# Two transpositions by DMA earlier on their queue, and one step's PSUM transposes later and copied by another engine

## The chip, the cores and the metric

The kernel runs on one core of one Trainium2 chip. The metric is the device time of one execution in microseconds (us). Before the change three executions took 198.18, 198.23 and 198.60 us, median 198.23.

## What is computed

A lightning attention block with decay, followed by a dense layer with a tanh GELU:

```python
# q, k, v: (4, 8, 768, 64); lam: (8,); blocks of 64 rows, kv_state starts at zero
intra = einsum('bhic,bhjc->bhij', qb, kb) * Dmask      # Dmask[i,j] = lam**(i-j), i >= j
intra = einsum('bhij,bhjd->bhid', intra, vb)
inter = einsum('bhid,bhde->bhie', qb * lam_pow, kv_state)
out[:, :, block] = intra + inter
kv_state = lam_block * kv_state + einsum('bhsd,bhse->bhde', kb * rev_pow, vb)
...
x = out.transpose(0, 2, 1, 3).reshape(3072, 512)
h = x @ w_in                                           # w_in: (512, 2048)
g = 0.5 * h * (1 + tanh(sqrt(2/pi) * (h + 0.044715 * h**3)))
result = g @ w_out                                     # w_out: (2048, 512)
```

Inputs and output are float32; the kernel computes in float16 with float32 accumulation.

## The kernel before

The attention is cut into 24 steps. A step is one batch, 256 rows and four of the eight heads; its three loads (q, k, v, 256 KB each) go out in `load_step` (L60, DMA at L70). `cast_q` (L277) scales the queries to float16 on VectorE (L282), `cast_k` (L290) casts the keys on ScalarE (L295), `scale_v` (L264) scales the values on GpSimd (L266). Queries and keys must then be transposed so that the head dimension lies on the partitions. Up to step 7 TensorE does that into a PSUM tile `Tps` (`stage_t`, L309, matmuls at L321), and ScalarE or VectorE copies it to `qkT` (L325 to L330). From step 8 on (`FIRST_DMA_T`) it is a transposing DMA on SP's queue (`transpose_dma`, L299, L303), which here is called T8, T9 and so on by its step.

`scores` (L344) computes a step's scores S (L350), `causal` (L356) masks them on VectorE into PT (L360). `products` (L365) makes the K products for the state (L385), those of PT with v (L400) and those with the state (L413, L422). `burst` (L437) does the same for two steps at once: scores of both (four PSUM banks), O products (L460, two banks), K products (L475, two banks, `K0` and `K1`), then the products with the state (L488, L498). `update` (L535) carries the state: t on VectorE (L547, L550), u on GpSimd (L558, L565). `x_out` (L514) takes the attention's result to `xT` on ScalarE (L527, L529).

The dense layer is cut into seven groups of steps and each group into pieces in a list `filler`: `mm1` (L609) makes `Hps` in PSUM (L613) and has ScalarE apply the GELU to `gT` (L617); `mm2` (L622) makes `O2ps` (L628), copied out by ScalarE (L636); later groups use `product` (L668, matmuls at L692) and `seven` (L778, L791) with sums on VectorE (L662). `fill(n)` (L958) issues the next n pieces.

The order of the work is written out by hand from L988 to L1190: each engine, and SP's queue of DMAs, works through its own instructions in that order (`pin` keeps it). `R(n, s)` (L962) issues the scores of step n with the products of steps n and s; `U(n)` (L984) the second state update. `fill` calls put dense pieces between them. From step 8 to 12 a loop over `FILL` (L1083) does this; `prep_qk(n + 2)` (L269) in it casts and transposes two steps ahead, and loads run up to four steps ahead. Behind the loop stand `burst((13, 14), (12,))`, with six dense `Hps` pieces between step 16's casts and it, and `burst((15, 16), (13, 14))`.

All PSUM tiles come from one pool of eight banks (`ps_M`, L55); a bank is given out again when the last reader of its former tile is done. The buffers of the loads are four per name (`ld`, L45), those of `qkT` five (`qkp`, L47).

Of the kernel before, what the change touches and what calls it, by code (L numbers as in the profile page):

```python
# [15 lines left out]
def kernel(  # L16
# [43 lines left out]
    def load_step(s, names="qkv"):  # L60
        b, r = divmod(s, 2 * NSB)
        sb, half = divmod(r, 2)
        ts = ld32.setdefault(s, [])
        for nm, src in (("q", q), ("k", k), ("v", v)):
            if nm not in names:
                continue
            t = ld.tile([P, HH, 2, D], FP32, tag=nm + "32", name=f"{nm}32_{s}")
            rows = src[b, half * HH : (half + 1) * HH, sb * SB : (sb + 1) * SB, :]
            queue = nc.scalar if (nm, s) == ("v", 0) else nc.sync
            pin(queue.dma_start(out=t[:].rearrange("p h j d -> p h (j d)"),  # L70
                                in_=rows.rearrange("h (p j) d -> p h (j d)", j=2)))
            ts.append(t)
# [71 lines left out]
    def sum_win(m, j, eng):  # L144

        if not wi_sum:
            wi_sum.extend(wst.tile([P, 2, 2, DFF // 2], FP16, tag=f"w{2 + i}", name=f"ws{i}")
                          for i in range(2))
        a, op, b = I_SUMS[m]
        cs, fs = slice(0, 2), slice(512 * j, 512 * j + 512)  # L150
        pin(eng.tensor_tensor(w_in_block(m, cs, fs), w_in_block(a, cs, fs),
                              w_in_block(b, cs, fs), op))
# [92 lines left out]
    def prep(s):  # L245
        prep_qk(s)
        prep_v(s)
# [16 lines left out]
    def scale_v(s):  # L264
        tv = a16p.tile([P, 2, HH, D], FP16, tag="v16", name=f"v16_{s}")
        pin(nc.gpsimd.tensor_tensor(wide(tv[:]), ld32[s][2][:], decay(dv, s), ALU.mult))  # L266
        a16[s] = a16[s] + (tv,)

    def prep_qk(s):  # L269
        cast_qk(s)  # L270
        transpose_dma(s)

    def cast_qk(s):
        cast_q(s)
        cast_k(s)

    def cast_q(s):  # L277
        q32 = ld32[s][0]
        tqk = a16p.tile([P, 2, 2, HH, D], FP16, tag="qk16", name=f"qk16_{s}")
        tq, tk = tqk[:, 0], tqk[:, 1]  # L280
        q_eng = nc.gpsimd if s == 3 else nc.vector
        pin(q_eng.tensor_tensor(wide(tq), q32[:], decay(dq, s), ALU.mult))  # L282
        if s == 0:
            inverse(halves[0])
            odd(halves[1])
            inverse(halves[1])
        a16[s] = (tq, tk)
        whole_qk[s] = tqk

    def cast_k(s):  # L290
        tk, k32 = a16[s][1], ld32[s][1]
        if s == 4:
            pin(nc.vector.tensor_copy(out=wide(tk), in_=k32[:]))
        else:
            pin(nc.scalar.activation(out=wide(tk), in_=k32[:], func=AF.Copy))  # L295
# [3 lines left out]
    def transpose_dma(s):  # L299
        tqk = whole_qk.pop(s)  # L300
        if s >= FIRST_DMA_T:
            o = qkp.tile([P, 2, 2, 2, P], FP16, tag="qkT", name=f"qkT_{s}")
            pin(nc.sync.dma_start_transpose(out=o[:].rearrange("p a j h t -> p (a j h) t"),  # L303
                                            in_=tqk[:].rearrange("p a j h d -> p (a j h d)")))
            qkT[s] = o
            if s == FIRST_DMA_T + 1:
                load_step(s + 1, "v")

    def stage_t(s):  # L309
        if s >= FIRST_DMA_T:  # L310
            return
        tq, tk = a16[s][:2]
        if s < 4:
            Tps = [ps_M.tile([P, 2, 2, P], FP16, tag="M", name=f"Tps{i}") for i in range(2)]
        else:
            Tps = ps_M.tile([P, 2, 2, 2, P], FP16, tag="M", name="Tps")
        for i, t in enumerate((tq, tk)):
            to = Tps[i] if s < 4 else Tps[:, i]
            for hp in range(2):
                for j in range(2):  # L320
                    pin(nc.tensor.transpose(to[:, j, hp, :], t[:, j, 2 * hp : 2 * hp + 2, :],  # L321
                                            ident[:]))
        o = qkp.tile([P, 2, 2, 2, P], FP16, tag="qkT", name=f"qkT_{s}")
        if s < 4:
            pin(nc.scalar.activation(out=o[:, 0], in_=Tps[0][:], func=AF.Copy))  # L325
            pin(nc.vector.tensor_copy(out=o[:, 1], in_=Tps[1][:]))
        elif s in (5, 6, 8):
            pin(nc.scalar.activation(out=o[:], in_=Tps[:], func=AF.Copy))
        else:
            pin(nc.vector.tensor_copy(out=o[:], in_=Tps[:]))  # L330
        qkT[s] = o
# [12 lines left out]
    def scores(n):  # L344
        o = qkT[n]
        Sps = [ps_M.tile([P, 2, 2, P], FP32, tag="M", name=f"S{hl}") for hl in range(2)]
        for hp in range(2):
            for jk in range(2):
                for hl, c in TILES:
                    pin(nc.tensor.matmul(  # L350
                        Sps[hl][half64(c), hp, jk, :], o[half64(hl), 1, jk, hp, half64(c)],
                        o[half64(hl), 0, :, hp, half64(c)], start=True, stop=True,
                        skip_group_check=True))
        Ss[n] = Sps

    def causal(n):  # L356

        t = ptp.tile([P, 2, 2, 2, P], FP16, tag="PT", name=f"PT_{n}")
        for hl, Sps in enumerate(Ss.pop(n)):
            pin(nc.vector.tensor_tensor(  # L360
                t[:, hl].rearrange("p b c d -> p b (c d)"), Sps[:].rearrange("p b c d -> p b (c d)"),
                mask[:].unsqueeze(1).to_broadcast([P, 2, 2 * P]), ALU.mult))
        PTs[n] = t
# [227 lines left out]
    def store_pair(pair):  # L591
        rows = out[2 * pair * P : 2 * pair * P + 2 * P, :].rearrange("(i p) d -> p i d", p=P)
        for i in range(2):
            pin(nc.sync.dma_start(out=rows[:, i], in_=o_pairs[pair][:, i]))
# [363 lines left out]
    def fill(n):  # L958
        for _ in range(min(n, len(filler))):
            filler.pop(0)()  # L960

    def R(n, s, ahead=None, keep=False):  # L962

        def first():
            if n is not None:
                scores(n)
            if ahead:
                ahead()

        if s in NARROW:  # L970
            products(n, s, between=first)
        else:
            first()
            products(n, s)
        if n is not None:
            causal(n)
        if s is not None and s % 2 == 1:
            g, i = group_of[s // 2]
            if i == len(groups[g]) - 1 and g > 0:
                queue_group(g)  # L980
        if n is not None and not keep:
            update(n, 0)

    def U(n):  # L984
        update(n, 1)


    idle(2, 512)  # L988
    prep(0)
    stage_t(0)  # L990
    chunk_decay()
    idle(1)
    prep(1)
    R(0, None)
    idle(0, 384)
    stage_t(1)
    idle(3)
    U(0)
# [3 lines left out]
    causal(1)  # L1002
    idle(2)
    stage_t(2)
    prep_qk(3)
    update(1, 0)
# [49 lines left out]
    sum_wout(1, 2, DVE)  # L1056
    fill(2)
    R(4, None)
    stage_t(5)
    U(4)  # L1060
    prep(6)
    fill(2)
    R(5, 4)
    stage_t(6)
    U(5)
# [18 lines left out]
    for n, (a, b, c, d) in FILL.items():  # L1084
        stage_t(n)
        fill(a + (n == 10))
        if n == 8:
            cast_q(n + 2)
            fill(1)
            cast_k(n + 2)  # L1090
            transpose_dma(n + 2)
        else:
            prep_qk(n + 2)
        if n < 11:
            load_step(n + 4, "qkv" if n < 10 else "qk")
        if n == 9:
            store_pair(1)
        if n == 11:
            scale_v(13)
            load_step(14, "v")  # L1100
            load_step(16, "qk")
        elif n == 9:
            scale_v(11)
        elif n == 10:
            scale_v(12)
            load_step(15, "qk")
        elif n == 12:
            scale_v(14)
        fill(b + (n == 8) - (n == 10))
        R(n, n - 1, keep=n == 8)  # L1110
        fill(c)
        if n == 8:
            update(n, 0)
            scale_v(n + 2)
            fill(2)
        U(n)
        if n == 12:
            prep_qk(15)
            load_step(15, "v")
            load_step(16, "v")  # L1120
            scale_v(15)
        fill(d)
        if n > 8:
            sum_win((n - 7) // 2, (n - 1) % 2, nc.vector)

    cast_qk(16)
    load_step(17, "qk")
    transpose_dma(16)
    load_step(17, "v")
    while kept_stores:  # L1130
        kept_stores.pop(0)()
    scale_v(16)
# [86 lines left out]
```

## Time and profile before

| What | Value |
|---|---|
| Time, median of three executions | 198.23 us (198.18 to 198.60) |
| Profiled execution | 198.31 us, its span 196.5 us |
| TensorE (PE) | 189.7 us busy, 97% of the span |
| VectorE (DVE) | 145.7 us, 74% |
| ScalarE (ACT) | 126.0 us, 64% |
| GpSimd (POOL) | 68.1 us, 35% |
| Mean granted TensorE clock | 0.997 of full speed |
| DMA | 38.13 MB, mean 194 GB/s |

The profile is of one execution on the chip; its times count from the start of the span. Lines as L613 are lines of the kernel. In a list by time each line has the start, the length, the engine, the operation with output and input, a count, and in brackets the engine's idle time before it with what ended that. SPq is the queue on which SP issues DMAs: its lengths are the time to issue, not to transfer; a transfer's end is its landing. The chain of waits is the work that ended last, followed back from the end; a list of waits gives, for an engine and line and what it waited for, the total in us, the number of times and the longest. Ends of matmuls are modelled, so that their starts say more than their busy share.

### The profile page before, as it was taken

What the parts mean: (1) busy time and instruction counts of PE and PEld (TensorE: products, weight loads), DVE (VectorE), ACT (ScalarE), POOL (GpSimd) and SP (SyncE); (2) the same over time, 40 slices, a digit from 0 to 9 for tenths busy, and PEclk for the clock granted to TensorE, in tenths of its full rate; (3) what the DMA queues carried; (4) which work ended last, traced back from release to release, by engine and by line L of the source; (5) the groups of instructions that cost most, each with busy time, mean ns of one, the idle gap of its engine ahead of it and who ended that gap; (6) DMA issues with size and microseconds to landing.
All of it is one profiled execution on the core that took longest, in us unless ns stands there. A gap on an engine that the chain in (4) does not pass through costs nothing.

```text
span 196.5 us, 5992 instructions
## 1 busy us (share of the span) xinstructions
PE 189.7 (97%) x2469; PEld 138.7 (71%) x2469; DVE 145.7 (74%) x291; ACT 126.0 (64%) x250; POOL 68.1 (35%) x85
## 2 busy tenths in 40 slices
PE   8878999999999999999999999999999999999992
PEld 2546544456888888654688754578888888888882
DVE  4987732889989879949889926999557996487520
ACT  3673778357774796686856379844877856678211
POOL 6594213557444732068524416064002030002000
PEclk9999999999999999999999999999999999999998
DMA  6999999999999999999997999600520300021105
GB/s 168 291 322 385 386 386 387 298 286 295 255 218 237 262 343 219 213 217 302 256 275 169 266 307 156 146 4 0 47 87 29 110 5 0 3 107 45 65 29 184
DMA packets 62810, 38.13 MB, mean 194 GB/s; under 512 B 18624, under 2 KB 55744, under 8 KB 62784
## 3 DMA queue, kind: packets, MB, share of 16 engines
q1 hardware_dynamic: 62240, 37.50, 76.8%
q8 instruction: 19, 0.31, 0.7%
q10 hardware_dynamic: 544, 0.26, 0.5%
q14 instruction: 7, 0.06, 0.1%
HBM read 27.26 MB, written 6.29 MB: 171 GB/s over the span
## 4 chain that ended last, share of the span: by engine, by line
PE 89%; SPq 4%; DMA 4%; ACT 0%; issue 0%
PE Hps L613 25%; PE MX L692 18%; PE MY L692 9%; PE HX L791 7%; PE O2ps L628 7%; PE MW L692 4%; DMA wi<-in_moe_w_in_dram 4%; SPq L70 4%; PE HY L791 4%; PE S L350 3%; PE Hps L890 3%; PE HW L791 2%; PE O L460 1%; PE OK L400 1%; PE Tps L321 1%; PE OK L422 1%
## 5 line engine op out<-in xcount | busy, mean ns | idle before, releaser
L613 PE MATMUL Hps<-xT,w_in 128*128 128x512 f16 (+1 forms) x288 | 50.5, 332 | 0.0
L613 PEld LDWEIGHTS <-w_in 128*128 128x128 f16 x288 | 27.8, 98 | 19.4
L617 ACT ACTIVATE gT<-Hps 128x512 f16<-128x512 f32 x56 | 32.6, 597 | 9.1 <-PE Hps L613 8.7
L360 DVE TENSOR_TENSOR PT<-S,mask 128x512 f16<-128x512 f32 x48 | 30.3, 680 | 8.6 <-PE S L350 8.6
L692 PEld LDWEIGHTS <-gs 128*128 128x128 f16 x320 | 31.1, 98 | 3.7
L266 POOL TENSOR_TENSOR v<-v,dv 128x512 f16<-128x512 f32 x24 | 27.5, 1150 | 17.3 <-DMA v<-in_v_dram 17.1
L692 PEld LDWEIGHTS <-gT 128*128 128x128 f16 x240 | 23.2, 98 | 3.5 <-ACT gT L617 0.2
L565 POOL TENSOR_TENSOR u<-t,lumask 128x256 f16<-128x256 f32 x21 | 15.2, 737 | 22.6 <-DVE t L550 13.6
L692 PE MATMUL MX<-w_sum,gs 128*128 128x256 f16 x160 | 21.4, 273 | 0.0
L662 DVE TENSOR_TENSOR gs<-gT 128x1024 f16<-128x1024 f16 (+1 forms) x24 | 17.2, 722 | 3.0 <-ACT gT L617 3.0
L282 DVE TENSOR_TENSOR qk<-q,dq 128x512 f16<-128x512 f32 x23 | 18.3, 798 | 1.2 <-DMA q<-in_q_dram 1.1
L295 ACT ACTIVATE qk<-k 128x512 f16<-128x512 f32 x23 | 14.4, 625 | 7.2 <-DMA k<-in_k_dram 7.1
L744 POOL TENSOR_TENSOR o<-u,q 128x512 f32<-128x512 f32 (+1 forms) x5 | 6.1, 1212 | 37.0 <-ACT u L709 37.0
L558 POOL TENSOR_TENSOR u<-t,lamu 128x128 f16<-128x128 f32 x19 | 10.7, 572 | 21.3 <-DVE t L550 15.7
L628 PE MATMUL O2ps<-w_out,gT 128*128 128x512 f16 x64 | 14.6, 379 | 0.0
L791 PEld LDWEIGHTS <-ws 128*128 128x128 f16 x128 | 12.4, 98 | 1.6 <-DVE xs L770 0.2
L529 ACT ACTIVATE xT<-OK 128x256 f16<-128x256 f32 x22 | 8.7, 453 | 6.7 <-PE OK L422 3.1
L709 ACT ACTIVATE u<-MX 128x256 f32<-128x256 f32 x18 | 6.9, 383 | 7.4 <-PE MX L692 7.4
L628 PEld LDWEIGHTS <-gT 128*128 128x128 f16 x64 | 6.1, 98 | 6.6
L692 PE MATMUL MY<-w_out,gs 128*128 128x256 f16 x80 | 10.7, 273 | 0.0
L805 DVE COPY u<-HX 128x512 f32<-128x512 f32 x8 | 5.5, 689 | 6.8 <-ACT gT L809 4.4
L692 PE MATMUL MX<-w_sum,gT 128*128 128x256 f16 x80 | 10.4, 273 | 0.0
(105 smaller groups left out, 322.0 us busy)
## 6 DMA issues: line engine op xcount, KB each, us to landing
q<-in_q_dram SPq DMA_DIRECT2D x24, 256.0 KB, 5.0
k<-in_k_dram SPq DMA_DIRECT2D x24, 256.0 KB, 5.1
v<-in_v_dram SPq DMA_DIRECT2D x23, 256.0 KB, 5.2
out_dram<-o SPq DMA_DIRECT2D x23, 256.0 KB, 4.1
wo<-in_moe_w_out_dram SPq DMA_DIRECT2D x4, 1024.0 KB, 9.5
wi<-in_moe_w_in_dram SPq DMA_DIRECT2D x4, 512.0 KB, 8.2
wi<-in_moe_w_in_dram SPq DMA_DIRECT2D x2, 1024.0 KB, 12.8
v<-in_v_dram ACTq DMA_DIRECT2D x1, 256.0 KB, 4.3
```

The lines of the kernel that those rows point to most:

```text
L266: pin(nc.gpsimd.tensor_tensor(wide(tv[:]), ld32[s][2][:], decay(dv, s), ALU.mult))
L282: pin(q_eng.tensor_tensor(wide(tq), q32[:], decay(dq, s), ALU.mult))
L295: pin(nc.scalar.activation(out=wide(tk), in_=k32[:], func=AF.Copy))
L360: pin(nc.vector.tensor_tensor(t[:, hl].rearrange("p b c d -> p b (c d)"), Sps[:].rearrange("p b c d -> p b (c d)"), mask[:].unsqueeze(1).t ...
L558: pin(nc.gpsimd.tensor_tensor(u, state[half][:], lamu[:, 2 * half : 2 * half + 2].unsqueeze(2).to_broadcast([P, 2, D]), ALU.mult))
L565: pin(nc.gpsimd.tensor_tensor(u[:], state[half][:].unsqueeze(2).to_broadcast([P, 2, 2, D]), lumask[:, 2 * half : 2 * half + 2, :].unsqueez ...
L613: pin(nc.tensor.matmul(by_block(Hps[:, i, :]), w_in16[:, c, f * P : (f + 1) * P], x(c), start=(c == 0), stop=(c == NC - 1)))
L617: pin(nc.scalar.activation(out=dst, in_=Hps[:], func=AF.Gelu_apprx_tanh))
L628: pin(nc.tensor.matmul(O2[tau][0][:], gT[:, f % HF, f // HF, tau * P : (tau + 1) * P], w_out16[:, f, :], start=(n == 0), stop=(n == NF - 1)))
L662: pin(nc.vector.tensor_tensor(g_rows(m, i), g_rows(a, i), g_rows(b, i), op))
L692: pin(nc.tensor.matmul(dst, lhsT, rhs, start=(opens and i == 0), stop=(closes and i == HF - 1), skip_group_check=True))
L791: pin(nc.tensor.matmul(dst[:, i, :], w_in_block(a, slice(c, c + 1), slice(f * P, f * P + P))[:, 0], x_block(b, slice(c, c + 1))[:, 0], sta ...
```

## The change

Two things are done.

First, step 5. Its transposes on TensorE (`stage_t(5)`) stood right behind `R(4, None)`, with two dense pieces between them and the scores of step 5 and none before. Now one of these two pieces stands ahead of the transposes and one behind. The copy of step 5's `Tps` to `qkT` goes from ScalarE (L328) to VectorE (L330). (Step 8, which the old condition named too, is transposed by DMA and does not come here.)

Second, SP's queue of DMAs. The load of q and k of step 16 was issued in the loop's round 11, behind the load of v of step 14; now it is issued in round 12, behind the transposition of step 14. And the transposition of step 16 stood behind the load of q and k of step 17; now it stands ahead of it, right behind the casts of step 16. On SP's queue:

```
before: T13, v14, q16, k16, T14, T15, v15, v16, q17, k17, T16, v17
after:  T13, v14, T14, q16, k16, T15, v15, v16, T16, q17, k17, v17
```

On ScalarE and VectorE the casts of steps 14 to 17 keep their places among the other instructions.

```diff
@@ stage_t
-        elif s in (5, 6, 8):
+        elif s == 6:
             pin(nc.scalar.activation(out=o[:], in_=Tps[:], func=AF.Copy))
         else:
             pin(nc.vector.tensor_copy(out=o[:], in_=Tps[:]))
@@ the order of the work
     R(4, None)
+    fill(1)
     stage_t(5)
     U(4)
     prep(6)
-    fill(2)
+    fill(1)
     R(5, 4)
@@ in the loop over FILL
         if n < 11:
             load_step(n + 4, "qkv" if n < 10 else "qk")
+        elif n == 12:
+            load_step(16, "qk")
...
         if n == 11:
             scale_v(13)
             load_step(14, "v")
-            load_step(16, "qk")
@@ behind the loop
-    cast_qk(16)
-    load_step(17, "qk")
-    transpose_dma(16)
-    load_step(17, "v")
+    prep_qk(16)
+    load_step(17)
```

## The prediction

> **What bounds the kernel now.** I read the page's chain first, then TensorE's waits, then the stretches that the change touches. A step is one q, k, v triple; T14 stands for step 14's transposition by DMA, S for scores.
>
> ```profile
> PE 89%; SPq 4%; DMA 4%; ACT 0%; issue 0%
> ```
>
> The chain is TensorE (PE) nearly throughout; the SP and DMA shares lie in the first 18 us. TensorE's waits:
>
> ```profile
> PE S L350 <- DVE qkT L326: 0.8, 2, 0.5
> ...
> PE OK L422 <- POOL u L565: 0.5, 1, 0.5
> ```
>
> These and the others listed lie before 20 us. From 20 to 193 us TensorE is busy without a break, so there is almost nothing for a reordering to gain, and any new stall is added to the end. The one trace of a wait is in the chain in order of time (start, length, what):
>
> ```profile
> 86.98 0.67 PE S L350 x32
> ...
> 87.88 0.28 PE K L475 x32
> ...
> 93.56 0.57 PE S L350 x32
> ```
>
> Both S lines are 32 equal matmuls, of steps 13/14 and 15/16. The first takes 0.10 more: between S13 and S14 the starts stand 120 ns apart where others stand 46. S14's weight loads begin at 87.24; T14's last semaphore increment is at 87.19. So T14 comes 0.07 us late. T16 landed at 92.59, 1.2 us before S16 needs it.
>
> ScalarE before that burst:
>
> ```profile
> 84.43 0.60 ACT L617 ACTIVATE gT<-Hps 128x512 f16<-128x512 f32 x1 [0.27 <-PE Hps L613]
> 85.03 0.63 ACT L295 ACTIVATE qk<-k 128x512 f16<-128x512 f32 x1
> 85.57 1.19 ACT L617 ACTIVATE gT<-Hps 128x512 f16<-128x512 f32 x2
> 87.02 0.60 ACT L617 ACTIVATE gT<-Hps 128x512 f16<-128x512 f32 x1 [0.27 <-PE Hps L613]
> ```
>
> The second line casts step 16's keys (k16). Three gelus are queued behind it. The last ends at 87.62, and the program's waits name it: K1, the second PSUM bank of the burst's K products (L475), is the bank that gelu empties. K starts at 87.71. That margin is 0.09 us, less the 0.05 that a release takes elsewhere (T14's increment to S14's load).
>
> SP's queue, and k16's landing counted from its issue:
>
> ```profile
> 76.00 3.43 SPq L303 DMA_TRANSPOSE qkT<-qk  x1
> 79.47 0.58 SPq L70 DMA_DIRECT2D v<-in_v_dram  x1
> 80.10 0.51 SPq L70 DMA_DIRECT2D q<-in_q_dram  x1
> 80.65 0.55 SPq L70 DMA_DIRECT2D k<-in_k_dram  x1
> 81.36 3.32 SPq L303 DMA_TRANSPOSE qkT<-qk  x2
> ```
>
> ```profile
> DMA to landing us min/median/max: 4.4/4.4/4.4
> ```
>
> The order is T13, v14, q16, k16, T14 and T15. k16 landed at 80.65 + 4.36 = 85.01 and its cast began at 85.03: ScalarE had no slack left for it. The DMA engines in these stretches (last two columns: DMA share, GB/s):
>
> ```profile
> 84.30:85.25 0.95, 0.95 (x6) 0.42 (x5) 0.74 (x1) 0.82 (x2) 0.95 (x2) 1.00 1.27 280
> ...
> 85.70:87.00 1.30, 1.30 (x12) 0.48 (x14) 0.00 (x0) 1.04 (x2) 0.86 (x2) 1.00 1.02 9
> 87.00:87.50 0.50, 0.50 (x36) 0.43 (x40) 0.12 (x1) 0.48 (x1) 0.00 (x0) 1.00 1.21 268
> ```
>
> T14's 256 KB move in the first stretch. T15 then moves half its packets and halts for 1.3 us, though it had been issued by 84.69. What precedes a halted transposition has its increments held too: T14, whose data had moved by 85.25, reports at 87.19; k15, just ahead of the halting T13, landed 6.2 us after its issue instead of 4.4. By their packets twelve of the sixteen transpositions halt so; T14, T16, T18 and T19 do not (first to last packet 1.0 to 1.9 us instead of 1.7 to 2.8).
>
> [...] landings follow SP's order, 0.85 to 0.95 us apart. [...] a cast that waits for its load holds the gelus behind it. The list above is consistent with that; no long such wait is in this stretch. [...]
>
> **Step 5's transposes later.** Eight transposes (L321) swap places with one piece of four O2ps matmuls (4 x 0.216 = 0.86 us): nothing is added on TensorE. The ScalarE copy (L328, 1.025 us) goes; VectorE gets a copy (L330) in its place:
>
> ```profile
> 41.92 1.27 DVE L360 TENSOR_TENSOR PT<-S,mask 128x512 f16<-128x512 f32 x2
> 43.12 0.46 DVE L550 SCALAR_TENSOR_TENSOR t<-t,lamu,OK 128x64 f32<-128x64 f32 x2
> 43.50 0.68 DVE L282 TENSOR_TENSOR qk<-q,dq 128x512 f16<-128x512 f32 x1
> ```
>
> ```profile
> L330 DVE COPY qkT<-Tps x2: 690/691/692, 39.8 to 50.7; 128x1024 f16<-128x1024 f16 x2
> ```
>
> The transposes now start near 42.75 and end near 43.36. VectorE, busy since 40.51, reaches the copy at 43.50, where step 6's query cast started. It ends at 44.19; a release takes 0.05 (the early copies of L326 show it), so S5 loads at 44.24 instead of 44.16: +0.08 us. Between 0 (were VectorE earlier) and 0.3. On VectorE step 6's cast and PT of step 5 follow some 0.2 to 0.7 late; 0.45 us of idle before PT takes up most. PT5's products are at 47.7, PT then ready at 46.1; step 6's transposes at 45.1, its queries then ready at 44.9. ScalarE's removed microsecond ends nobody's wait.
>
> **Transpositions sooner.** T14 is issued after v14, at 80.10 instead of 81.36, ahead of q16 and k16; its casts were done at 79.76. On the compute engines no instruction of these steps changes place, on GpSimd's queue nothing at all; v15, v16 and T15 keep theirs on SP. T14 lands before 86 or so: S14's 0.07 us go. T16 passes q17 and k17, and T16's input depends on k16. S16 had 1.2 us of slack; q17 and k17 slip by about 1 us, and their casts stood at 92.53 (landed 90.92) and 94.09 (landed 91.78): covered, still more so if TensorE is late.
>
> The cost: k16 is now behind T14 in the ring, so its data come at least one transposition (0.95 us) later. They then take the place directly ahead of T15, which T14 held. The DMA total up to there is unchanged. If T15 halts as before, k16 reports when T14 did, at 87.19. ScalarE then casts at 87.2; from cast start to the end of the third gelu are 0.54 + 3 x 0.60 = 2.34 us, so K1's bank is free at 89.54 and K1 starts at 89.59 instead of 87.71: +1.88 us. S5's 0.08 disappears in this wait, because the DMA sets its end. O1 and K0 wait for the first two of these gelus and come in under it. Nothing later gives it back, TensorE having no idle.
>
> The sum is made against the profiled execution: 198.31 us, of which 196.5 are its span and 1.8 lie around it. 198.31 + 1.9 = 200.2. The median shown is 0.08 lower: 200.1.
>
> **Rivals.** (a) Likeliest: exactly one of T14 and T15 halts ahead of k16's report; 200.1, bounds 199.6 to 200.6; 0.44. (b) Both halt: for it, twelve of sixteen halt and T14 now starts closer behind its issue; against it, T14 did not. k16 then reports 1.3 us later still: 201.4; 0.22. (c) Neither: k16 at 85.96, K1 at 85.98 + 2.34 + 0.05 = 88.37: +0.66, 198.9; 0.11. (d) T13 does not halt or the whole DMA stream runs about 1.3 us earlier: k16 reports by 85.3, and the third gelu is again held by its matmuls only: 198.1 to 198.5; 0.17. (e) The other side: T14's lateness is the point. In the trace it costs 0.07 us; were T14 commonly late by a further halt (1.3 us, TensorE waiting from 87.15 on), its removal would give 196.9 to 197.8. It decides from a T14 landing after 87.5. Against it, profiled and unprofiled times differ by only 0.08 us; 0.06.
>
> **How the numbers follow.** Some 0.2% (0.4 us) is about what can be told from no change. Slower: (a), (b), (c), 0.77. Same: (d), 0.17. Faster: (e), 0.06. The likeliest case is 200.1. The range goes from the middle of (d), 198.3, to that of (b), 201.4; it leaves out (e), half of (d) and the upper part of (b), together 0.2. The halt is the unknown cost, 0 or 1.3 us for each of two transpositions, and I take one.
>
> **What would show it.** Right: on ScalarE a wait of about 2 us for k at L295 near 85; K at L475 starting near 89.6; S of steps 13/14 down to 0.57 in the chain; S5 some 0.1 late. Wrong: the cast of k16 starting by 85.3, or TensorE passing K without a gap. The whole is wrong if the gelu that K1 waits for was issued ahead of the cast.

## The result, and the profile after

The changed kernel takes 200.59 us, the median of six executions (199.93 to 202.29), beside 198.34 for the kernel before (six, 198.17 to 198.60). The ratio is 1.013 (95% interval 1.0088 to 1.0173): slower, clear of the noise. A second set of six, e8_after below, gave 201.24 (200.02 to 202.39), ratio 1.014 (1.0101 to 1.0179). The ratios in this document leave out executions over 1.5% above the fastest of their kernel, one of e3_t16 and four of e5_v15_between. The profiled execution took 200.44 us, 2.13 more than that of before; its span is 198.7.

The page's chain, after:

```profile
PE 87%; DMA 5%; POOL 2%; SPq 2%; ACT 1%; issue 1%; ACTq 0%; POOLq 0%
```

TensorE lost two points of the chain. POOL's share lies in the first 14 us; where the kernel differs, the chain in order of time (start, length, what) is:

```profile
82.73 4.97 DMA k<-in_k_dram
...
87.72 0.63 ACT qk L295
88.35 1.47 ACT gT L617 x3
...
89.86 0.44 PE K L475 x31
...
95.70 0.57 PE S L350 x32
```

The chain no longer runs through TensorE here. It runs from the load of k16 to its cast, through the three gelus behind the cast, and to the K product that needs the bank of the third. K1 starts at 89.86, not 87.71: +2.15. The scores of steps 15/16 start at 95.70, not 93.56: +2.14. In this execution the distance stays from here to the end; nothing is given back. ScalarE's list says the same:

```profile
87.72 0.63 ACT L295 ACTIVATE qk<-k 128x512 f16<-128x512 f32 x1 [1.89 <-DMA k<-in_k_dram]
88.26 1.55 ACT L617 ACTIVATE gT<-Hps 128x512 f16<-128x512 f32 x3
```

The bracket is the idle time ahead of the cast, ended by the load. Before, this cast began at 85.03 with none. TensorE's list at the same place, before and then after:

```profile
86.91 0.74 PE L350 MATMUL S<-qkT 64*64 64x128 f16 x32
87.48 0.39 PE L460 MATMUL O<-PT,v 64*64 64x128 f16 x16
87.71 0.45 PE L475 MATMUL K<-v,qk 64*64 64x64 f16 x32
```

```profile
87.71 0.64 PE L350 MATMUL S<-qkT 64*64 64x128 f16 x32
88.18 0.22 PE L460 MATMUL O<-PT,v 64*64 64x128 f16 x1
88.89 0.41 PE L460 MATMUL O<-PT,v 64*64 64x128 f16 x15 [0.49 <-ACT gT L617]
89.37 0.18 PE L475 MATMUL K<-v,qk 64*64 64x64 f16 x1
89.86 0.44 PE L475 MATMUL K<-v,qk 64*64 64x64 f16 x31 [0.30 <-ACT gT L617]
```

Three waits, one for each gelu: ahead of O1 (the first O matmul, on the other bank, is at 88.18, the next at 88.89), ahead of K0 (0.24 by the starts, under the list's threshold) and ahead of K1. The 32 scores of 13/14 run on without a break: S14's wait is gone.

SP's queue, after:

```profile
76.44 3.42 SPq L303 DMA_TRANSPOSE qkT<-qk  x1
79.91 0.58 SPq L70 DMA_DIRECT2D v<-in_v_dram  x1
80.65 1.41 SPq L303 DMA_TRANSPOSE qkT<-qk  x1
82.10 0.58 SPq L70 DMA_DIRECT2D q<-in_q_dram  x1
82.73 0.53 SPq L70 DMA_DIRECT2D k<-in_k_dram  x1
83.92 1.24 SPq L303 DMA_TRANSPOSE qkT<-qk  x1
```

The order is T13, v14, T14, q16, k16, T15, as the change says. Landings by the completion increments (a DMA here has sixteen): T14 84.46, q16 85.60, k16 87.70, T15 88.60. Those of k16, directly ahead of T15, which halts:

```
86.27 86.37   87.55 87.58 87.62 87.63 87.64 87.64 87.65 87.66 87.66 87.67 87.67 87.68 87.69 87.70
```

By the DMA packets of this trace T15's halted ones (nineteen of 256 bytes that take 0.7 to 1.5 us each, where most take 0.02) begin at 86.02 to 86.87 and end at 87.55 to 87.58. Two increments come while they stand, fourteen as they end or after. The data were done well before: the trace has sixteen packets of 4 bytes at the end of each load, as many as it has increments, and k16's are at 85.52 to 85.88. The increments of q16, one load ahead, follow such packets by 0.5 to 0.7 us; the fourteen of k16 follow by 1.7 us and more.

This execution has one disturbance of its own: from 14.71 us TensorE ran at half clock (0.50) for 3.41 us and was some 0.8 us late from there to the burst. The wait for k16 took that up, because a DMA sets its end, so that only 0.49 us of wait is left ahead of O1 where e2_t14 and e8_after show 1.2.

### The profile page after: what moved, and what is told of

The parts are those of the page before. It is cut to its first block, busy times and chain, and to the rows that moved or that the text cites. A ratio compares the mean times of both kernels' runs of the same rounds, so it can differ in the third digit from the quotient of the medians.

```text
span 198.7 us, 5991 instructions
## 1 busy us (share of the span) xinstructions
PE 191.2 (96%) x2467; PEld 139.6 (70%) x2469; DVE 145.6 (73%) x292; ACT 124.3 (63%) x249; POOL 67.5 (34%) x85
## 4 chain that ended last, share of the span: by engine, by line
PE 87%; DMA 5%; POOL 2%; SPq 2%; ACT 1%; issue 1%; ACTq 0%; POOLq 0%
PE Hps L613 22%; PE MX L692 17%; PE MY L692 9%; PE HX L791 7%; PE O2ps L628 7%; PE MW L692 4%; PE Hps L890 4%; PE HY L791 4%; PE S L350 3%; DMA v<-in_v_dram 3%; DMA k<-in_k_dram 3%; PE HW L791 2%; PE OK L400 2%; SPq L70 1%; PE Tps L321 1%; PE O L460 1%
## 5 line engine op out<-in xcount | busy, mean ns | idle before, releaser
L266 POOL TENSOR_TENSOR v<-v,dv 128x512 f16<-128x512 f32 x24 | 28.8, 1203 | 16.5 <-DMA v<-in_v_dram 14.2
L662 DVE TENSOR_TENSOR gs<-gT 128x1024 f16<-128x1024 f16 (+1 forms) x24 | 18.0, 759 | 3.8 <-ACT gT L617 3.8
L744 POOL TENSOR_TENSOR o<-u,q 128x512 f32<-128x512 f32 (+1 forms) x5 | 5.6, 1121 | 37.0 <-ACT u L709 37.0
L558 POOL TENSOR_TENSOR u<-t,lamu 128x128 f16<-128x128 f32 x19 | 9.4, 501 | 22.0 <-DVE t L550 16.3
L350 PEld LDWEIGHTS <-qkT 64*64 64x64 f16 x384 | 6.4, 108 | 6.0 <-DVE qkT L326 2.1
```

The costliest lines, as they stand in the source:

```text
L350: pin(nc.tensor.matmul(Sps[hl][half64(c), hp, jk, :], o[half64(hl), 1, jk, hp, half64(c)], o[half64(hl), 0, :, hp, half64(c)], start=True, ...
L662: pin(nc.vector.tensor_tensor(g_rows(m, i), g_rows(a, i), g_rows(b, i), op))
```

## The experiments

None of these kernels leaves out part of the computation. The short diffs are against the kernel after. The kernel before was run beside them: median 198.33 in the first set (e1 to e4, 35 executions), 198.34 in the second (e5 to e8, 43). The last three (e9 to e11) are single profiled executions, with one of the kernel before (198.51).

**e1_step5: the part on step 5 alone.** SP's queue as before:

```diff
-        elif n == 12:
-            load_step(16, "qk")
...
             load_step(14, "v")
+            load_step(16, "qk")
...
-    prep_qk(16)
-    load_step(17)
+    cast_qk(16)
+    load_step(17, "qk")
+    transpose_dma(16)
+    load_step(17, "v")
```

> Step 5's part alone, SP's queue as before. If the loss comes from ScalarE's wait for k16 (theory), this part costs the 0.08 us of S5's wait at most: 198.3 to 198.5, with the cast of k16 starting near 85.0. If VectorE's extra 0.69 us copy is the cause (rival), most of the 2.2 us shows here: over 200.

Measured: 198.28 us, ratio 0.999 (0.9978 to 1.0002). ScalarE at the burst is as before:

```profile
85.05 0.63 ACT L295 ACTIVATE qk<-k 128x512 f16<-128x512 f32 x1
```

Step 5's part makes no measurable difference.

**e2_t14: T14 sooner alone.** Step 5, and T16 behind q17 and k17, as before:

```diff
-        elif s == 6:
+        elif s in (5, 6, 8):
...
-    fill(1)
     stage_t(5)
     U(4)
     prep(6)
-    fill(1)
+    fill(2)
...
-    prep_qk(16)
-    load_step(17)
+    cast_qk(16)
+    load_step(17, "qk")
+    transpose_dma(16)
+    load_step(17, "v")
```

> T14 sooner alone (q16 and k16 behind it); step 5 and T16 as before. Theory: all of the loss, 200.2 to 200.8, the cast of k16 starting after 87 and K1's matmuls near 89.6. Rival (step 5's copy, or T16 passing q17 and k17): 198.3 to 198.6.

Measured: 199.95 us (199.82 to 202.08), ratio 1.0091 (1.0059 to 1.0124). ScalarE's list, and TensorE's waits in this stretch (total, times, longest):

```profile
87.53 0.63 ACT L295 ACTIVATE qk<-k 128x512 f16<-128x512 f32 x1 [2.58 <-DMA k<-in_k_dram]
```

```profile
PE O L460 <- ACT gT L617: 1.2, 1, 1.2
PE K L475 <- ACT gT L617: 0.3, 1, 0.3
```

k16 landed at 87.50 and K1 starts at 89.67. Most of the loss comes with this one move: 1.62 us by the medians, a little under the expected 200.2 to 200.8, against 2.25 for the whole change. Step 5's and T16's parts cost nothing by themselves (e1, e3). Of the 0.6 between, the profiles show 0.2 to 0.3: in those of the changed kernel k16 lands at 87.70 and 87.82, with T13's first packet, ahead of all that was moved, at 79.70 and 79.78 instead of 79.49. Half clocks (e8 below) come on top; the rest is open.

**e3_t16: T16 sooner alone.**

```diff
-        elif s == 6:
+        elif s in (5, 6, 8):
...
-    fill(1)
     stage_t(5)
...
-    fill(1)
+    fill(2)
...
-        elif n == 12:
-            load_step(16, "qk")
...
             load_step(14, "v")
+            load_step(16, "qk")
```

> T16 sooner alone (q17 and k17 behind it); the rest as before. Theory: no change, 198.2 to 198.5, since S16 had 1.2 us to spare and the casts of step 17 some more. Rival (the queue behind T16 gets late and holds something on): over 199.5.

Measured: 198.40 us, ratio 1.0002 (0.9992 to 1.0012); one of fourteen executions, 202.91 at a mean granted clock of 0.948, has no explanation. T16 landed at 90.94, q17 at 91.91, k17 at 93.19, and TensorE shows no wait from 60 to 120 us: covered.

**e4_k16_late: all of the change, but k16's cast behind the three gelus.** This is the test of the mechanism. The load stays as late; only what is queued behind its cast changes.

```diff
-    prep_qk(16)
+    cast_q(16)
+    fill(3)
+    cast_k(16)
+    transpose_dma(16)
     load_step(17)
...
-    fill(3)
     burst((13, 14), (12,))
```

> The changed kernel with one ScalarE instruction moved: the cast of k16 stands behind the three gelus that it stood ahead of, and T16 behind it; SP's order as in the changed kernel. Theory: the gelus no longer wait for the load, K0 and K1 get their banks at 87.6, and the loss goes although k16 lands just as late: 198.2 to 198.7. Rival (the DMA stream or T14's early place costs by itself): still 200.2 or more.

Measured: 198.37 us, ratio 1.0003 (0.9992 to 1.0013). ScalarE's list:

```profile
85.19 0.60 ACT L617 ACTIVATE gT<-Hps 128x512 f16<-128x512 f32 x1 [0.27 <-PE Hps L613]
86.06 0.60 ACT L617 ACTIVATE gT<-Hps 128x512 f16<-128x512 f32 x1 [0.27 <-PE Hps L613]
86.92 0.60 ACT L617 ACTIVATE gT<-Hps 128x512 f16<-128x512 f32 x1 [0.27 <-PE Hps L613]
87.82 0.63 ACT L295 ACTIVATE qk<-k 128x512 f16<-128x512 f32 x1 [0.30 <-DMA k<-in_k_dram]
```

k16 landed at 87.80, later than in the kernel after, and the loss is gone. So lateness of k16 costs nothing by itself; its place ahead of the gelus in ScalarE's queue does. It also shows what T14 sooner is worth: the scores of 13/14 take 0.57 us in the chain instead of 0.67, and S15/16 start at 93.41 instead of 93.56 (0.10 of this TensorE had ahead of the burst already). But the MX products at 98.56 then take 1.88 us instead of 1.75, and at the scores of 116.20 the two kernels are 0.01 apart. What those products wait for was not tried; four gelus run on ScalarE there.

**e5_v15_between: v15's load between k16 and T15**, so that T15's halt should hold v15 and not k16.

```diff
         if n == 12:
-            prep_qk(15)
             load_step(15, "v")
+            prep_qk(15)
             load_step(16, "v")
```

> The changed kernel with v15's load moved ahead of T15 on SP's queue, so that v15 and not k16 stands directly ahead of T15. Theory (T15's halt holds k16's report): k16 is reported some 0.9 us after q16, near 86.1, its cast starts there, and K1 comes some 0.8 us late: 198.9 to 199.5; v15 is held in its place. Rival (k16 is late merely for standing behind T14, T15 has no part): the cast of k16 still starts after 87 and the time is that of the changed kernel, 200.0 to 200.7.

Measured: median 198.55 us of 22 executions (198.28 to 202.76), ratio 1.0022 (1.0003 to 1.0041). k16 landed at 86.14, 0.88 after q16; v15 was held, to 88.81. K1 waits 0.2 only:

```profile
86.17 0.63 ACT L295 ACTIVATE qk<-k 128x512 f16<-128x512 f32 x1 [0.79 <-DMA k<-in_k_dram]
```

The hold moved to the DMA in between, as expected. The median is below the expected 198.9 to 199.5, in part since gelus that are queued up run 0.475 us apart and not 0.60 (three take 1.55): K1 comes 0.60 us late here (88.31) and 0.31 in e10 (88.02), instead of 0.8. But the times lie in three heaps: 15 at 198.3 to 198.9, three at 200.2 to 200.8, four at 202.0 to 202.8. Two more profiled executions of it take this up.

**e10_v15_again and e11_v15_again2: the same kernel, two more profiles.**

> The same kernel as e5_v15_between, one more profiled execution. Of its 22 times 15 lay within 198.3 to 198.9, three at 200.2 to 200.8 and four at 202.0 to 202.8. Theory: in most executions k16 is reported near 86.1 and costs 0.2; in some it is held like in the changed kernel, to some 87.5 to 87.8, which gives 200.2 or so, and a lower granted clock behind the wait gives 202 (the mean clock of those four was 0.988 to 0.991). So the profile shows k16's cast at 86.2 with 198.3 to 198.9, or at 87.5 to 87.8 with 200.2 and more. Rival: the slower executions lose their time elsewhere; then the cast is at 86.2 with a time above 200.

> As e10_v15_again, a third profiled execution of the same kernel: k16's cast at 86.2 with 198.3 to 198.9, or at 87.5 to 87.8 with 200.2 and more; by the rival the cast is at 86.2 with a time above 200.

Measured: 198.46 and 200.29 us. ScalarE in e10, then in e11:

```profile
85.88 0.63 ACT L295 ACTIVATE qk<-k 128x512 f16<-128x512 f32 x1 [0.88 <-DMA k<-in_k_dram]
```

```profile
87.72 0.63 ACT L295 ACTIVATE qk<-k 128x512 f16<-128x512 f32 x1 [2.73 <-DMA k<-in_k_dram]
```

Each cast starts where its time asks for it, so the rival (a loss elsewhere) falls. But what kept k16 back in e11 was not T15's halt. Its increments, e10 above e11:

```
85.58 85.62 85.63 85.64 85.64 85.65 85.66 85.67 85.67 85.71 85.74 85.79 85.81 85.83 85.84 85.86
85.79 85.82 85.83 85.83 85.84 85.85 85.86 85.86 85.87 85.93 86.01 86.06 86.09 86.10 86.18   87.69
```

In e11 fifteen were in by 86.18 and one came at 87.69. T15's halted packets end there at 88.34 to 88.38, and v15, directly ahead of it, reports from 88.42 on, as a held DMA does; k16's last increment does not wait for that. Its own data were late by what the packets show. Fifteen of k16's closing packets of 4 bytes come by 85.71, the sixteenth at 86.88. A 16 KB packet of the queue of instruction packets (q8, "instruction", on the page) runs from 85.60 to 86.61. On its end follow, one behind another, five packets of 512 bytes, the closing one at 86.88, and then 32 of 512 bytes and v15's closing packet at 87.94. The trace kept here does not number the DMA engines; by the order of its packets the author takes these for the end of one engine's share of k16 and all of its share of v15. In e10 a like packet runs from 85.13 to 86.45, and only v15's 32 follow: by the same reading that engine had done its share of k16.

So in e11, by this reading, the loss came by chance, from an instruction packet in front of the end of one engine's share. The increment followed its closing packet by 0.81 us where the other fifteen took 0.5 to 0.6; these last 0.2 us are open. That e5's other slow executions have the same cause is likely, not shown.

**e6_before_v15: the kernel before with v15's load ahead of T15**, to free T14 from the hold.

> The kernel before with v15's load moved ahead of T15, so that v15 stands between T14 and T15. Theory: T14 is reported near 86.1 instead of 87.2 without having been moved, S14 waits no more, the 32 score matmuls of steps 13 and 14 take 0.57 instead of 0.67 in the chain; the time gains at most 0.1 us, 198.1 to 198.5. Rival (T14's late report has to do with T14's own place): S14 still waits; also no measurable change, so the trace decides.

Measured: 198.23 us, ratio 0.9997 (0.9984 to 1.001). The expectation on T14 missed: fifteen of its increments came by 86.10, the sixteenth at 87.61. As for k16 in e11, an instruction packet (85.51 to 86.50) is in front by the order of the packets: the late engine's closing packets of T14 are at 86.48 and 86.50, the others' at 85.47 to 85.54. T15's halted packets end only at 88.11 to 88.15, so their halt did not hold it; why its increment followed by 1.1 us and not by 0.6 is open. S14 stood behind another releaser in this execution:

```profile
PE S L350 <- ACT gT L617: 0.3, 1, 0.3
```

**e7_k16_ahead: the change with k16 ahead of T14 and only q16 behind it.**

```diff
         elif n == 12:
-            load_step(16, "qk")
+            load_step(16, "q")
+            ld32[16].reverse()
...
             load_step(14, "v")
+            load_step(16, "k")
```

> The changed kernel with k16's load back ahead of T14; only q16's stays behind T14, directly ahead of T15. Theory: k16 is reported before 85.3 and ScalarE loses nothing, but q16 is held till after 87; VectorE's cast of it then stands ahead of PT of step 13, which frees the PSUM bank of the first dense piece behind the burst: that piece, at 88.2 before, starts near 89.2, 199.0 to 199.6. Rival (only ScalarE's gelus matter): 198.2 to 198.5.

Measured: 198.95 us, ratio 1.003 (1.002 to 1.0039), just below what was expected. k16 landed at 84.36; now q16 takes the hold, to 87.57. In this execution TensorE was some 0.7 us late ahead of the burst, which hid the wait; one more profiled execution shows it:

**e9_k16_ahead_again.**

> The same kernel as e7_k16_ahead, one more profiled execution. There TensorE was some 0.7 us late by 84 us, which hid the place of the loss. If the loss is q16's report, held by the transposition behind it, then in an execution that is on time at 84 us VectorE casts q16 near 87.6, PT of step 13 follows, and TensorE stands at the O products for VectorE for about 0.5 us; time 198.7 to 199.3. Rival: q16 costs nothing and the loss lies in front of 84 us; then no wait shows at the burst and VectorE's cast of q16 ends in time.

Measured: 198.84 us. The chain:

```profile
82.22 5.17 DMA q<-in_q_dram
...
87.41 0.69 DVE qk L282
88.10 0.61 DVE PT L360
...
88.76 5.34 PE Hps L613 x24
```

q16's cast on VectorE holds PT of step 13, and TensorE stands 0.49 us for it: the wait and its size as expected, though not at the O products but at the first dense piece behind the burst. The same hold, one engine further: where it lands decides who is late.

**e8_after: the changed kernel again.**

> The changed kernel once more, beside the three others on the same chip. Theory: 200.0 to 200.8, cast of k16 starting between 87.2 and 87.9, TensorE waiting for ScalarE within the burst for 1.3 to 2 us in all. Open: whether the first microseconds, where the first profile of it was 0.8 us late, repeat; if they don't, all of the loss should stand at the burst.

Measured: 201.24 us (200.02 to 202.39), ratio 1.014 (1.0101 to 1.0179), above the expected 200.0 to 200.8; the profiled execution took 202.22. The chain:

```profile
82.80 5.02 DMA k<-in_k_dram
...
87.85 0.63 ACT qk L295
88.48 1.47 ACT gT L617 x3
...
89.99 0.44 PE K L475 x31
90.43 0.22 PE O L498 x2
90.65 6.87 PE Hps L613 x24
97.51 0.57 PE S L350 x32
```

K1 comes 2.28 late. But the 24 dense matmuls behind it take 6.87 us, where e4 and before (the line below) take 5.18 for the same work, and that is another 1.7.

```profile
88.38 5.18 PE Hps L613 x24
```

The table of stretches of e8 (its last three columns are granted clock, DMA share and GB/s) and the page's clock row (40 slices, tenths of full speed) show where:

```profile
87.41:90.82 3.41, 1.85 (x80) 1.26 (x69) 2.76 (x6) 2.58 (x6) 1.02 (x2) 1.00 1.13 258
90.50:95.00 4.50, 4.50 (x16) 1.67 (x15) 2.00 (x8) 1.69 (x4) 2.77 (x6) 0.62 0.97 271
```

```profile
PEclk9999999999999999996999999999999999999999
```

TensorE's clock was granted at half from 90.82, for 3.41 us. The stretches of one clock in this trace last 85.33, 3.41 and 105.81 us, which are 25, 1 and 31 times 3.413; in the trace shown first 10.24, 3.41 and 180.91 us are 3, 1 and 53 times. In the interval of that length ahead, 87.41 to 90.82, TensorE was busy for 1.85 us and idle for 1.56. In e11, if intervals of 3.413 us are counted through, the stall fell across the end of one, 1.40 us in one, and no half clock followed; in e2's profile 1.11 and none. That the idle of one such interval brings half clock in the next is the author's reading of these traces; no run was made to show it.

Every execution's mean granted clock agrees with half clock as the cause of the times near 202, though it does not tell where a half clock fell. Of the 18 of the changed kernel and e2, five have 0.990 or 0.991 and 201.97 to 202.39 us (202.29, 202.22, 202.39, 201.97 and, in e2, 202.08); the profile shown first also has 0.991, but there the half clock came ahead of the burst and was swallowed. The other twelve are at 199.82 to 200.62 but for one of 201.84, at 0.997, which stays open. e5's four above 202 have 0.988 to 0.991. Of the 78 of the kernel before one has 0.991 (198.79 us) and none less; one of e3, at 198.74, has 0.991 too.

## Why the prediction was right, point by point

**Step 5.** Predicted +0.08 us for S5, absorbed at the burst. VectorE's copy, after:

```profile
43.84 0.46 DVE L550 SCALAR_TENSOR_TENSOR t<-t,lamu,OK 128x64 f32<-128x64 f32 x2
44.22 0.68 DVE L330 COPY qkT<-Tps 128x1024 f16<-128x1024 f16 x1
44.82 0.81 DVE L282 TENSOR_TENSOR qk<-q,dq 128x512 f16<-128x512 f32 x1
```

It stands where forecast, between t and step 6's query cast. S5's first matmul starts 0.35 us after the last one of the piece ahead, instead of 0.31: 0.04 us. e1 confirms that it costs nothing.

**T14's lateness.** Right in place: S14's wait is gone in every kernel that has T14 sooner. Read as 0.07 us from the starts in the profile of before; in e1's the same wait is 0.21 (255 ns between the starts of S13 and S14 instead of 46), and still worth nothing at the end, as e4 shows. Rival (e), a gain, falls with e4.

**T16.** Predicted covered, and it is (e3).

**The cost.** The mechanism is the one forecast: k16 behind T14, held by T15's halt, its cast holding three gelus, the third emptying K1's bank. e2 has it alone, e4 takes it away by moving the cast. Case (a), exactly one transposition halts, is what both traces of the changed kernel show: T14's packets take 0.97 and 0.98 us, T15's 2.51 and 2.49. Case (d) did not come: T13 halted in every trace. k16's data did come behind T14's: its closing packets are at 85.52 to 85.88, those of before at 84.28 to 84.34.

Two terms of that sum were off, in opposite directions. k16 was to report at 87.19 and did so at 87.70: T15's first packet came at 85.52 instead of 85.23, with the stream late already (T13 was issued at 76.44, not 76.00), and T15 took 2.51 us instead of 2.29: together 0.29 + 0.22 = 0.51, and the cast began at 87.72 instead of 87.2: +0.52. From the cast's start to K1's were to be 2.34 + 0.05 and were 2.14, since gelus that are ready run 0.475 apart: -0.25. So K1 at 89.59 + 0.52 - 0.25 = 89.86, where it is. That the second takes back half of the first is luck.

**The sum.** 200.2 was forecast against the profiled execution's 198.31; the changed kernel's took 200.44. Without a half clock behind the burst the other executions of the changed kernel lie at 199.9 to 200.6 (but for the 201.84), around the forecast of 200.1 with the 0.3 more of the two terms. What the sum lacks is a term: "Nothing later gives it back" fits, but a later loss can be added to it. In e8's trace half clock behind the stall cost 1.7 us, and by the mean clock five of eighteen executions are likely to have had one there. A stall of 2.16 us (87.83 to 89.99 in e8) lies whole within one interval of 3.41 in (3.41 - 2.16) / 3.41 = 37% of cases, six or seven of eighteen. This is an estimate from these two lengths in e8's trace; it takes it that the intervals run on evenly and that the stall must lie whole within one, which was not tried. The executions at 202 lie above the range that the prediction gave; three of them in e8's set lift its median to 201.24.

**"Directly ahead."** The prediction said that a halting transposition has the DMA ahead of it held, and no trace goes against it: in all thirteen the DMA directly ahead of T15, be it T14, k16, q16 or v15, has fourteen or more of its sixteen increments at the end of T15's halted packets or behind it. The single late increments two places ahead (e6, e11) are read as another thing, an instruction packet in front of one DMA engine's share (85.51 to 86.50 and 85.60 to 86.61). The trace of before had one already: fifteen increments of q15, two places ahead of T13, came by 79.10 and the sixteenth at 80.55, in the midst of T13's halt (79.75 to 81.24), with an instruction packet from 77.57 to 78.77. Such a packet is a term that the prediction did not have; it did not decide the changed kernel's time.

**ScalarE's order.** That a cast that waits for its load holds the gelus queued behind it was only consistent with the trace of before. e4 against the kernel after shows it: k16 landed as late (87.80 and 87.70), the order in ScalarE's queue was the other, and the times are 2.2 us apart (198.37 and 200.59).

## What to carry to other kernels

Before a load is moved back on a queue of DMAs, look at what stands behind its consumer: here 2.2 us hung not on k16, which had nobody waiting for it, but on three gelus queued behind its cast. The DMA directly in front of the transposition that halts reported only when the halt was over (k16 at 87.70, T15's halted packets ending at 87.55 to 87.58), so such a landing is to be forecast from the halt and not from the DMA's own bytes. Where one increment of sixteen is late (e11: 87.69, the others by 86.18), look for another queue's packet in front of that one's share before blaming the neighbour. And a stall of TensorE may cost more than its own length: in e8 one of 2.16 us was followed by half clock that cost 1.7 more.

## What the runs showed of the hardware that was not expected

- In e8 the granted clock fell to half for 3.41 us after an interval of that length with 1.56 us of TensorE idle (1.7 us lost); 1.40 us of idle (e11) did not do it, nor 1.36 from 10.1 us on in e2. In the profile shown first 1.30 us did, from 11.3 us on, so idle time alone does not set the point.
- The halt went with the step, not the neighbours: in all thirteen traces T14 and T16 never halted and T13 and T15 always did (first to last packet 0.96 to 1.45 us against 2.28 to 2.91), whether T14 follows v14 or k16, and whether k16 or v15 stands ahead of T15. Why was not found.
- The halt held increments, not data: in e8 k16's closing packets are at 85.63 to 85.69, T15's halted packets end at 87.65 to 87.69, and fifteen of k16's increments come at 87.73 to 87.82 (one at 86.51).
- In e11 a 16 KB instruction packet (85.60 to 86.61) stood, by the order of the packets, in front of the rest of one DMA engine's share of a load: k16's sixteenth closing packet came at 86.88, the others by 85.71.
- Gelus of 128x512 took 0.60 us each but started 0.475 us apart where they were queued up: 1.55 us for three (the kernel after, from 88.26).
